# Emission times of the attention scores: two neighbouring groups at one time, from batch 3 on

## The chip, the cores and the metric

The kernel runs on one core of one Trainium2 chip. The metric is the device time of one execution in microseconds (us). The engines are TensorE (PE; its weight loads are shown apart as PEld), VectorE (DVE), ScalarE (ACT), GpSimd (POOL) and SyncE (SP), whose queue issues most of the transfers.

## The reference

Input: q, k, v of shape 8 x 8 x 576 x 64 (batches, heads, positions, head size), and two weights, 512 x 2048 and 2048 x 512. Everything is float32.

```python
scores = scale * q @ k.T                       # per batch and head, 576 x 576
scores = where(0 <= s - t < 128, scores - slope[h] * (s - t), -1e9)
attn = softmax(scores) @ v                     # window of 128 keys, one slope per head
x = heads side by side                         # 8 x 576 x 512
u = x + real(fft(fft(x, axis=1), axis=2))
un = (u - mean(u)) / sqrt(var(u) + 1e-6)       # over the last axis
out = u + max(un @ w_ch1, 0) @ w_ch2
```

## The kernel before

The work of a batch has three stages: attention, the Fourier stage with the normalization (`fourier`, `norm`), and the two FFN products (`ffn`). Three batches are in flight: while the attention of batch b runs, the FFN of batch b - 2 gives TensorE its bulk.

**Attention.** The heads are taken in pairs, four pairs a batch; p = 4b + j counts them through, 0 to 31. The window of 128 keys leaves five tiles of query rows (`TILES`), which form three groups (`SGRP`): group 0 has tiles 1 and 0, group 1 tiles 3 and 2, group 2 tile 4. `scores(p, i)` (line 378) computes group i. From batch 2 on (`NF` = 2) each product of float32 is made of three float16 products, so that a group has 12, 12 or 6 matmuls. Each of them contracts over 64 rows: one head of the pair lies in the upper 64 rows of the array and the other in the lower 64, and they write two PSUM banks, `sp0` and `sp1`. All other matmuls of these batches use the full 128 rows. Pool `ps_s` has two buffers of each bank, that is, two pairs of banks. The other four banks are two for the FFN (`fp`), one for the output of the attention (`pv`) and one for the Fourier stage (`pd`).

Behind a group come, for each of its tiles and heads: a VectorE instruction that adds the bias, masks and takes the row minimum into `nb` (line 391; it is what frees the score bank, and there are four, four or two of them in a group); the exponential on ScalarE; in `halves`, a float16 copy on ScalarE (line 404) and the remainder on VectorE; and in `flip`, a DMA transpose into `pt` on SP's queue (line 413). The tiles `P` have 9 buffers, `pt` 6. `values(p, i, e)` (lines 445 to 447) multiplies `pt` of one head and group with v, and `weigh` divides by the row sum. `convert` makes the float16 halves of q, k and v ahead of a pair.

**FFN.** For each block of 256 positions (odd batches have a third block of 128), FFN1 (line 699) fills an `fp` bank with 24 matmuls of 256 columns (48 of 128 in the small block); ScalarE (line 704) and then VectorE (a helper, line 158, into `hbuf`) take it out and so free the bank. FFN2 (line 713) then runs 48 matmuls of 512 columns for each output tile. `ffn` is a generator that is resumed in 64 steps a batch (80 in odd batches).

**Order.** The order is written as due times: `put(t, f, ...)` lays a call into a heap, `after(dt, ...)` one behind the present time, and the loop at the end takes them out in order of time (calls of one time in the order in which they were put), which is the order of emission. A batch has 24 units of time and a head pair 6. In units from a pair's begin, t: its scores at 0, 2 and 4, its `values` at 5.66 to 10.66, one by one; what follows `scores` is emitted 0.25 to 0.85 units behind it. The FFN of batch b - 2 begins 0.4 units behind the begin of batch b and alternates FFN1 and FFN2 in halves of 6 units (in odd batches 4.8, with the small block at the end). Then the framework's planner goes over the emitted instructions with a simulated clock: on each engine it takes the earliest emitted one whose inputs and buffers are ready by that clock, and so may put a later one ahead. The engines run the planned order strictly, with semaphores for what must wait.

Of the kernel before, what the change touches and what calls it, by code (L numbers as in the profile page):

```python
# [22 lines left out]
NF = 2  # L23
# [32 lines left out]
def begin_of(p):  # L56
    return 6 * PACE[0] * p if p < 4 else T1 + 6 * (p - 4)
# [6 lines left out]
def forward_of(b):  # L64
    return transform_of(b) + (START - DFT if b else 11 * PACE[1])
# [11 lines left out]
def attn_fft_ffn_kernel(  # L77
# [76 lines left out]
    def put(t, f, *a):  # L154
        heappush(queue, (t, next(order), f, a))
# [567 lines left out]
    for p in range(4 * B):  # L723
        b, j = divmod(p, 4)
        t, f = begin_of(p), 1 if b else PACE[0]
        put(t - 7 * f if p else -3.2, load, p)
        if b < NF:
            put(t - 3.8 * f if p else -2, convert, p, 0)
            put(t - 1.2 * f, load_v, p)
            put(t + 4.2 * f, v_max, p)  # L730
        else:
            early = p < 4 * NF + 2
            put(t - (1.3 if early else 6.8), load_v, p)
            for what, x in enumerate((4.6, 3.6, -2 if early else 1.2)):
                put(t - x, convert, p, what)
        for i in range(3):
            put(t + 2 * i * f, scores, p, i)
            for e in range(2 if b < NF else 0):
                put(t + (2 * i + e + LB + 0.33) * f, turn, p, i, e)
        for x in range(6):  # L740
            put(t + (x + LC + 0.66) * f, values, p, x % 3, x // 3)
        if b < NF and j == 3:
            put(t + 5 * f, f32_scale, b)
# [5 lines left out]
    for b in range(B):  # L749
        t = begin_of(4 * b)  # L750
# [4 lines left out]
        t = forward_of(b)  # L755
# [88 lines left out]
def program(q, k, v, moe_w_ch1, moe_w_ch2):  # L844
    import numpy as np
    import concourse.bacc as bacc

    B = q.shape[0]
    qa = np.ascontiguousarray(q.transpose(0, 1, 3, 2)[..., query_order()]).reshape(B, 4, 128, NQ)
    ka = np.concatenate([k, k[:, :, :NK - S]], axis=2).transpose(0, 1, 3, 2)  # L850
    ka = np.ascontiguousarray(ka).reshape(B, 4, 128, NK)
    idx = np.array([[min(s + p, S - 1) for s in VSTART] for p in range(128)])
    va = np.ascontiguousarray(v[:, :, idx])
    nf = min(B, NF)
    v0 = np.ones((nf, H, 128, 5, 65), np.float32)
    v0[..., 0:D] = va[:nf]
    w1 = np.ascontiguousarray(moe_w_ch1.reshape(4, 128, 16, 128).transpose(1, 2, 0, 3).reshape(128, -1))
    w2 = np.ascontiguousarray(moe_w_ch2.reshape(16, 128, DM).transpose(1, 0, 2).reshape(128, -1))
    w1, w2 = w1.view(np.int64), w2.view(np.int64)
    rel, slope, tab1, tab2 = tables()  # L860
    nc = bacc.Bacc("TRN2", target_bir_lowering=False, num_devices=1, dynamic_dma_scratch_size=1024)
    arrays, args = {}, []
    for name, a in (("q", qa), ("k", ka), ("v", va), ("v0", v0), ("w1", w1), ("w2", w2), ("rel", rel),
                    ("slope", slope), ("tab1", tab1), ("tab2", tab2)):
        arrays[name + "_dram"] = a
        args.append(nc.dram_tensor(name + "_dram", a.shape, mybir.dt.from_np(a.dtype), kind="ExternalInput").ap())
    rows = B * S
    args.append(nc.dram_tensor("out_dram", (rows, DM), F32, kind="ExternalOutput").ap())
    with tile.TileContext(nc, schedule_with_timeline_sim=True) as tc:
        attn_fft_ffn_kernel(tc, *args)  # L870
    return nc, arrays, B
```

## Time and profile before

| | |
|---|---|
| median of 3 runs | 1116.77 us (1116.02 to 1118.63) |
| the profiled execution's own time | 1116.72 us |
| span of its profile, first to last instruction | 1114.9 us |
| mean granted TensorE clock | 0.972 |
| busy: PE, DVE, ACT | 1069.6, 712.8, 580.8 us |
| score matmuls (L378), all batches | 880 |
| score reads on VectorE (L391), batches 2 to 7 | 240 |

The profile shows one execution. "L378" is line 378 of the kernel. Busy time of PE is modelled at the ends of matmuls, which are pipelined: two matmuls that follow each other overlap in their rows, so what one costs is read from the start of the next. In rows of waits, the instruction on the left waited for the one behind the arrow. In rows of the time order, "x12" means twelve like instructions merged into one row, with the first one's start and the time to the last one's end; a bracket holds the engine's idle time before it. "out<-in" are the program's tile names, without buffer numbers.

### The profile page before, as it was taken

The page shows a single profiled execution, that of the slowest core. Times are in us where ns is not written, and L with a number is a line of the kernel's source. Part 1 is how long each engine was busy: PE and PEld are TensorE (multiplying, and loading weights), DVE is VectorE, ACT ScalarE, POOL GpSimd, SP SyncE. Part 2 cuts the span into 40 slices and gives each one's busy share as a digit, 9 for nine tenths or more (in the row PEclk, how much of TensorE's full clock was granted, in tenths as well). Part 3 has the DMA queues.
Part 4 walks back from the last instruction along what each step waited for, and adds up shares of the span by engine and source line. Part 5 has one row for each costly group of instructions (what it writes and reads, how often), then busy time and mean ns, then how long its engine had stood idle before and what let it go on. Part 6 is the DMA issues. An engine that isn't in the chain of part 4 may idle for free.

```text
span 1114.9 us, 23952 instructions
## 1 busy us (share of the span) xinstructions
PE 1069.6 (96%) x9296; PEld 737.2 (66%) x9296; DVE 712.8 (64%) x2081; ACT 580.8 (52%) x1380; POOL 20.3 (2%) x59
## 2 busy tenths in 40 slices
PE   6999989879699999999999999999999999999998
PEld 4667768465374857767667677585758577767665
DVE  6988678815966667777868485869685655262111
ACT  5757889647863555446645464456635441151000
POOL 0000000000000000000000000000000000010000
PEclk9999859999899999999999999999999999999999
DMA  9941558656775235432642154344532240020000
GB/s 367 341 153 44 172 131 205 162 156 158 202 145 133 68 82 112 88 97 50 131 106 78 44 110 98 92 77 101 115 83 44 53 89 1 20 48 20 19 11 20
DMA packets 191507, 117.83 MB, mean 106 GB/s; under 512 B 154400, under 2 KB 164128, under 8 KB 191392
## 3 DMA queue, kind: packets, MB, share of 16 engines
q1 hardware_dynamic: 190816, 114.84, 40.8%
q8 instruction: 73, 1.20, 0.5%
q10 hardware_dynamic: 576, 1.45, 0.3%
q14 instruction: 42, 0.34, 0.1%
HBM read 70.63 MB, written 9.44 MB: 72 GB/s over the span
## 4 chain that ended last, share of the span: by engine, by line
PE 69%; DMA 7%; DVE 6%; ACT 3%; issue 1%; SPq 1%; ACTq 0%; DVEq 0%
PE fp L699 29%; PE fp L713 29%; PE sp L378 4%; PE pd L555 2%; DMA pt<-P 2%; DMA wall<-v_dram 2%; DMA wall<-q_dram 2%; ACT wall L257 1%; PE pd L589 1%; PE pv L445 1%; DMA wall<-k_dram 1%; PE pv L447 1%; PE pv L446 1%; DVE P L391 1%; DMA uT<-un 1%
## 5 line engine op out<-in xcount | busy, mean ns | idle before, releaser
L713 PE MATMUL fp<-wall,hbuf 128*128 128x512 f16 x1728 | 397.1, 383 | 2.4 <-DVE hbuf L158 2.3
L699 PEld LDWEIGHTS <-wall 128*128 128x128 f16 x3840 | 340.1, 99 | 61.3 <-issue 14.5
L699 PE MATMUL fp<-uT,wall 128*128 128x256 f16 x3072 | 364.8, 276 | 14.0 <-DVE hbuf L158 8.3
L713 PEld LDWEIGHTS <-hbuf 128*128 128x128 f16 x1728 | 163.2, 99 | 187.2 <-issue 11.5
L158 ACT ACTIVATE P<-P,nb 128x256 f32<-128x256 f32 x320 | 142.9, 479 | 124.6 <-DVE nb L391 124.5
L158 DVE SCALAR_TENSOR_TENSOR hbuf<-fp,hbuf 128x512 f16<-128x512 f32 x144 | 99.0, 688 | 130.4 <-ACT hbuf L704 130.0
L704 ACT ACTIVATE hbuf<-fp 128x512 f16<-128x512 f32 x144 | 85.1, 591 | 186.7 <-PE fp L699 186.5
L391 DVE CUSTOM_DVE_ANT_0 P<-sp,rg,nsl 128x256 f32<-128x256 f32 x240 | 97.3, 450 | 59.7 <-PE sp L378 51.9
L158 DVE SCALAR_TENSOR_TENSOR P<-P 128x256 f16<-128x256 f32 x240 | 88.6, 390 | 26.9 <-ACT P L404 25.6
L378 PE MATMUL sp<-kk,qq 64*128 64x256 f16 (+5 forms) x880 | 93.4, 294 | 11.5 <-DVE nb L391 5.9
L404 ACT ACTIVATE P<-P 128x256 f16<-128x256 f32 x240 | 86.0, 384 | 7.6 <-DMA pt<-P 7.0
L257 ACT ACTIVATE wall<-wall 128x512 f32<-128x512 f32 (+2 forms) x90 | 54.6, 606 | 49.5 <-DMA wall<-v_dram 19.2
L445 PE MATMUL pv<-vhs,pt 128*128 128x65 f16 x432 | 55.5, 195 | 4.6 <-DMA pt<-P 3.4
L446 PE MATMUL pv<-vl,pt 128*128 128x64 f16 x432 | 56.0, 193 | 0.0
L447 PE MATMUL pv<-vhs,pt 128*128 128x65 f16 x432 | 55.9, 194 | 0.0
L158 DVE SCALAR_TENSOR_TENSOR X<-fp,misc,X 128x512 f32<-128x512 f32 x32 | 23.8, 744 | 44.7 <-PE fp L713 44.7
L378 PEld LDWEIGHTS <-qq 64*128 64x128 f16 (+1 forms) x720 | 32.3, 100 | 28.5 <-issue 24.9
L445 PEld LDWEIGHTS <-pt 128*128 128x128 f16 x432 | 41.1, 98 | 15.0 <-issue 4.5
L299 PE MATMUL fp<-tab_sb 128*128 128x512 f16 x180 | 45.5, 379 | 1.1 <-DMA tab_sb<-tab_dram 1.1
L699 PE MATMUL fp<-wall,wall 128*128 128x128 f16 x768 | 45.4, 219 | 0.1
L446 PEld LDWEIGHTS <-pt 128*128 128x128 f16 x432 | 40.7, 99 | 7.0
L440 PE MATMUL pv<-vr,pt 128*128 128x65 f32 x288 | 41.3, 294 | 0.3 <-ACT pt L426 0.3
(146 smaller groups left out, 1200.4 us busy)
## 6 DMA issues: line engine op xcount, KB each, us to landing
qr<-q_dram SPq DMA_DIRECT2D x32, 304.0 KB, 3.1
hbuf<-w_dram SPq DMA_DIRECT2D x16, 512.0 KB, 7.2
out_dram<-X SPq DMA_DIRECT2D x32, 256.0 KB, 2.2
wall<-v_dram SPq DMA_DIRECT2D x30, 256.0 KB, 2.9
vr<-v_dram SPq DMA_DIRECT2D x24, 320.0 KB, 3.6
kr<-k_dram SPq DMA_DIRECT2D x24, 289.0 KB, 3.4
wall<-q_dram SPq DMA_DIRECT2D x24, 256.0 KB, 2.9
wall<-k_dram SPq DMA_DIRECT2D x24, 256.0 KB, 2.9
```

What stands on the lines that cost most here:

```text
L158: put(now[0] + dt, lambda: f(*a, **kw))
L257: A.activation(t, t, AF.Square, accum_out=box["mx"][:, i, c:c + 1])
L299: T.matmul(spin, trig[:, 0:128], trig[:, 0:512], start=True, stop=True)
L378: T.matmul(sp[e][:m, col:col + n], qq[h, c0:c0 + m], keys(kk[h], ti), start=(x == 0), stop=(x == len(prods) - 1))
L391: V.tensor_tensor_reduce(pt[:m, 0:n], sp[e][:m, col:col + n], tab[:m, pc:pc + n], mul, 3.0e38, ALU.add, ALU.min, nb[:m, ti:ti + 1])
L404: A.activation(hi, P32, AF.Copy, scale=2.0 ** 14)
L445: T.matmul(pv[:, ti], ph, vh[:, e, vc], start=first, stop=False)
L446: T.matmul(pv[:, ti, 0:D], ph, vl[:, e, vc], start=False, stop=False)
L447: T.matmul(pv[:, ti], pl, vh[:, e, vc], start=False, stop=last)
L699: T.matmul(fp[:, i * n:(i + 1) * n], w1_ap(e, c, f0 + i), uT[:, j, c, 0:n], start=(c == 0 and p == 0), stop=(c == 3 and p == 2))
L704: A.activation(ht[:, 0], fp, AF.Relu)
L713: T.matmul(op, hh[f][:, a, i * 128:(i + 1) * 128], w2_ap(e, f), start=(f == 0 and p == 0), stop=(f == 15 and p == 2))
```

## The change

```diff
         for i in range(3):
-            put(t + 2 * i * f, scores, p, i)
+            put(t + 2 * i * f + (0 if b < NF + 1 else 1 - 2 * ((3 * p + i) % 2)), scores, p, i)
             for e in range(2 if b < NF else 0):
                 put(t + (2 * i + e + LB + 0.33) * f, turn, p, i, e)
```

From batch 3 on (p = 12), the groups are numbered through as 3p + i. An even group's due time moves one unit later and an odd group's one unit earlier. The groups lay two units apart, so an even group and the odd one behind it now have the same due time: groups 0 and 1 of an even pair p at t + 1, its group 2 and group 0 of pair p + 1 at t + 5, groups 1 and 2 of pair p + 1 at t + 9 (t is the begin of pair p). At these times the even group is emitted first and the odd one directly behind it. What `scores` sends behind itself with `after` moves with it. `values`, `convert`, the loads and the FFN steps keep their due times. 60 groups make 30 such places.

## The prediction

> **What bounds the kernel now.** I read the page first (busy shares and the 40 slices), then stretches of the span, then TensorE's own waits, and only then the order of its instructions.
>
> ```profile
> PE 1069.6 (96%) x9296; PEld 737.2 (66%) x9296; DVE 712.8 (64%) x2081; ACT 580.8 (52%) x1380; POOL 20.3 (2%) x59
> ...
> PE   6999989879699999999999999999999999999998
> ...
> PEclk9999859999899999999999999999999999999999
> ```
>
> TensorE is at nine tenths or more in nearly all slices, against mean shares of 64% and 52% for VectorE and ScalarE. The slices in which PE falls short lie in the first third. Batch 3, where the change begins, starts its scores at 295 us, so the stretches from there on matter (columns: PE, PEld, DVE, ACT and POOL busy, granted clock, DMA share, GB/s):
>
> ```profile
> 299.00:303.00 4.00, 1.43 (x6) 0.86 (x6) 4.00 (x14) 4.00 (x11) 1.22 (x1) 0.53 0.90 259
> 303.00:310.00 7.00, 5.61 (x35) 4.13 (x36) 5.00 (x18) 4.18 (x11) 0.55 (x2) 0.54 1.15 237
> ...
> 340.00:600.00 260.00, 260.00 (x2421) 175.32 (x2420) 188.04 (x561) 133.16 (x317) 4.99 (x12) 1.00 0.41 92
> 600.00:860.00 260.00, 258.71 (x2501) 181.63 (x2500) 184.98 (x550) 136.53 (x322) 4.73 (x11) 1.00 0.39 87
> ```
>
> Two regimes. From 340 us on PE is busy without a hole at the full clock; VectorE has 72% and ScalarE 51% of the stretch. From 299 to 303 us VectorE and ScalarE are full instead, PE starves, and the granted clock stays near 0.53 until 310. TensorE's waits, first for 340 us to the end, then for 295 to 345 us (total us, times, longest), say the same:
>
> ```profile
> PE fp L699 <- DVE X L158: 0.8, 1, 0.8
> PE pv L445 <- DVE X L463: 0.3, 1, 0.3
> PE fp L699 <- DVE hbuf L158: 0.2, 1, 0.2
> ```
> ```profile
> PE sp L378 <- DVE nb L391: 4.9, 1, 4.9
> PE fp L713 <- DVE hbuf L158: 2.3, 1, 2.3
> PE fp L699 <- DVE hbuf L158: 1.9, 2, 1.3
> ```
>
> 1.3 us of waits in 775 us. So in the long stretch only less work for TensorE can shorten the kernel, and "busy" hides what it loses between instructions. That is read from starts. TensorE's order in time (start, duration of the merged row):
>
> ```profile
> 425.02 0.83 PE L378 MATMUL sp<-kk,qq 64*128 64x256 f16 x12
> 425.79 2.85 PE L699 MATMUL fp<-wall,wall 128*128 128x128 f16 x48
> ```
> ```profile
> 436.89 1.46 PE L713 MATMUL fp<-wall,hbuf 128*128 128x512 f16 x6
> 438.28 0.50 PE L378 MATMUL sp<-kk,qq 64*128 64x256 f16 x6
> 438.72 1.47 PE L713 MATMUL fp<-wall,hbuf 128*128 128x512 f16 x6
> 440.02 1.15 PE L699 MATMUL fp<-uT,wall 128*128 128x256 f16 x9
> ```
>
> Six L713 followed by other full-array work take 440.02 - 438.72 = 1.30 us; six followed by scores (L378, 64 rows of the array) take 438.28 - 436.89 = 1.39: 0.09 us on entering. Six scores take 0.44 us until the next instruction, twelve 0.77 (425.02 to 425.79): six more cost 0.33, so 0.11 us of a visit belongs to no matmul, the way out. One visit to the scores costs about 0.09 + 0.10 = 0.19 us (0.20 by the rounded rows; I take the smaller).
>
> [...]
>
> **The change part by part.** No instruction is added or removed: the score matmuls (30 for each head pair, 600 in batches 3 to 7) and what follows them stay. For these batches (20 head pairs, 60 groups) the even-numbered groups are emitted one unit later and the odd ones one earlier, so that two meet at one time, every four units, without other work emitted between them. A unit is 4.92 us here: the first scores of head pairs 16 and 24, 48 units apart, start at 442.92 and 679.00 us.
>
> ```profile
> 295.45 0.67 PE L378 MATMUL sp<-kk,qq 64*128 64x256 f16 x12
> ```
> ```profile
> 442.92 0.28 PE L378 MATMUL sp<-kk,qq 64*128 64x256 f16 x1
> 443.13 2.79 PE L699 MATMUL fp<-uT,wall 128*128 128x256 f16 x24
> 445.86 0.50 PE L378 MATMUL sp<-kk,qq 64*128 64x256 f16 x6
> 446.57 1.47 PE L699 MATMUL fp<-uT,wall 128*128 128x256 f16 x12
> 447.98 0.34 PE L378 MATMUL sp<-kk,qq 64*128 64x128 f16 x5
> ```
> ```profile
> 679.00 0.28 PE L378 MATMUL sp<-kk,qq 64*128 64x256 f16 x1
> ```
> ```profile
> 912.07 0.50 PE L378 MATMUL sp<-kk,qq 64*128 64x256 f16 x6
> ```
>
> *Visits.* Counted along PE's time order, the 600 scores of the 60 groups make 79 visits, the first at 295.45 and the last at 912.07. They are not 60, because the planner cuts groups: the rows show one group of 12 run as 1, 6 and 5, with 24 matmuls (one whole `fp` bank of FFN1 work) and 12 between the pieces. When a bank is not yet free in the plan, scores fill the hole, and older work takes TensorE back. 19 groups are cut, into 21 extra pieces (two neighbours already touch). After the change there are 30 places. If cuts fall by group they halve (41 visits); if they go with the bank changes that a piece of scores meets, all 21 stay (51 visits). The unit arithmetic favours the second: FFN1 and FFN2 halves alternate every 6 units (4.8 in odd batches), and the new places, at 1, 5 and 9 of every 12 units, fall into FFN1 halves two times in three, the groups of before about half the time. I take 51: 28 visits fewer x 0.19 = **-5.3 us**. Bounds: 30 visits (49 x 0.19 = -9.3) and 79 (0). Odd pieces leave one head's half of the array alone; that stays with the cuts, nothing.
>
> *Score banks.* Two buffers of each of `sp0`, `sp1`: a group reuses the banks of the group two before it, four units earlier, as now (19.7 us against the 1.7 us in which VectorE reads a group out, the four rows below), so the second group of a place finds its banks free: nothing. One exception: (12, 1) comes three units after (11, 2) instead of four, and just there PE waits the 4.9 us quoted, with the clock halved. Bounds: that wait vanishes, since the neighbour is emitted with other work now, -4.9; or grows by a whole unit, +4.9. I take 0, since VectorE, which sets it, is full in that stretch with either order.
>
> *Evictions.* Behind a place stand up to eight score reads (L391) on VectorE instead of four, then twice the exponentials on ScalarE, and behind those the evictions of `fp`.
>
> ```profile
> 457.33 0.47 DVE L391 CUSTOM_DVE_ANT_0 P<-sp,rg,nsl 128x256 f32<-128x256 f32 x1
> ...
> 458.54 0.48 DVE L391 CUSTOM_DVE_ANT_0 P<-sp,rg,nsl 96x256 f32<-96x256 f32 x1
> ```
> ```profile
> 443.03 0.60 ACT L704 ACTIVATE hbuf<-fp 128x512 f16<-128x512 f32 x1 [0.48 <-PE fp L699]
> ```
> ```profile
> 443.90 0.68 DVE L158 SCALAR_TENSOR_TENSOR hbuf<-fp,hbuf 128x512 f16<-128x512 f32 x1
> ```
>
> Four reads run from 457.33 to 459.02; four more cost 4 x 0.40 = 1.6 us of VectorE. An `fp` bank is full after 2.6 us (443.13 to 445.86, less the way in); the one full at about 443.0 is free at 444.58, so 1.0 us are spare. If a burst falls wholly on an eviction, PE waits 1.6 - 1.0 = 0.6 us; in 20 places of 30 (those in FFN1 halves) that is +12, the upper bound. Today bursts of four make 0.2 us of this wait in 775 us, and ScalarE and VectorE have 49% and 28% free; nearest to that row I take **+1.0 us** for all new short waits. Less than nothing has no reason here.
>
> *What hangs on the scores.* The exponential, the split and the transposes on SP's queue go with each group: 200 transposes, one unit earlier or later past the loads of q, k and v on the same queue.
>
> ```profile
> 463.83 0.51 PE L378 MATMUL sp<-kk,qq 64*128 64x256 f16 x6
> ```
> ```profile
> 468.55 2.85 SPq L413 DMA_TRANSPOSE pt<-P  x2
> ```
> ```profile
> L413 SPq DMA_TRANSPOSE pt<-P x190: 1167/1200/2446, 350.4 to 916.6; - x190
> ...
> DMA to landing us min/median/max: 2.3/2.4/5.7
> ```
>
> The tightest user is `values` of group 2 of an even head pair: 2.66 units (13.1 us) behind its scores instead of 3.66. The chain took 468.55 + 2.85 + 2.4 - 463.83 = 10.0 us: covered by 3.1. If not, `values` comes later in the plan and FFN matmuls fill in. The largest place queues 8 x 1.2 = 9.6 us of transposes, half of the 19.7 us to the next. `pt` has six buffers and was exactly full; now the last tile of a place waits until `values` frees one, 0.8 unit (4.0 us) later, eight units ahead of its own use. What stands behind it on SP is loads for a head pair not yet begun. All this at nothing; the cost if the cover is gone is a wait of PE of those same 3 to 4 us, once or twice.
>
> **Sum.** The profiled execution took 1116.72 us (span 1114.9, 1.8 around it), the median is 1116.77, so nothing is to be shifted. 1116.7 - 5.3 + 1.0 = **1112.4 us**.
>
> **The rivals.**
> - *More than that* (0.14): cuts halve (38 visits saved, -7.2) and the 4.9 us wait goes: 1104.6. For it: both halves of a place sit in one piece of emission. Against it: FFN1 halves and a full VectorE.
> - *It does not do what it says* (0.17): the planner, which put one group into three pieces, takes the places apart by bank and head, say 70 visits: -1.7, 1115.0, no change that shows. Against it: two groups in three are whole now.
> - *Slower by bursts* (0.16): the 0.6 us above at 20 places, +12, gives 1116.7 - 5.3 + 12 = 1123.4; it outweighs the gain from 0.27 us a place on. For it: places move into the FFN1 halves. Against it: the 0.2 us row. [...]
> - *Slower at the entry* (0.08): (12, 1) waits a unit longer for its bank, +4.9, and the clock stays near 0.53 for as long again, which costs 0.47 x 4.9 = 2.3 of the pace: 1112.4 + 7.2 = 1119.6. The rows at 299 to 310 us speak for it. Against it: the wait is set by VectorE's backlog, not by the place of the scores. [...]
>
> **How the numbers follow.** The forecast holds 0.45, its own range 1109.0 to 1114.5. About 0.2%, 2.2 us, is what a measurement of this kernel tells from no change. Faster: 0.45 + 0.14 = 0.59. Same: 0.17 and a mild form of the bursts, 0.02. Slower: 0.14 + 0.08 = 0.22. From 1104, just under the better case, to 1121, past the entry case, about 0.15 is left out, mostly the full burst case.
>
> **What would show it.** Right: about 50 visits of L378 from batch 3 on, most with 18 or 24 matmuls. L391 in runs of six to eight; the wait for `hbuf` from 340 us on below 2 us; PE at the full clock from 340 us on. Wrong: a row "PE fp L699 <- DVE hbuf L158" of 5 us or more (bursts); 65 visits or more (the planner); a longer "PE sp L378 <- DVE nb L391" with a clock near 0.5 after 310 us (the entry). The forecast fails most easily in the count of cuts and in the 295 to 340 us stretch, where PE waits in any case and a small shift of order can move several us either way.

## The result: slower by 1.3%, and the profile after

| | before | after |
|---|---|---|
| median | 1116.72 us (1116.02 to 1118.63) | 1131.23 us (1129.84 to 1131.86) |
| ratio, 95% interval | | 1.0126 [1.0108, 1.0143] |
| profiled execution, its span | 1116.72, 1114.9 us | 1130.83, 1129.0 us |
| mean granted clock | 0.972 | 0.974 |
| visits to the scores from batch 3 on | 79 | 51 |

The forecast was 1112.4 us with a range up to 1121.0. The kernel lies above both.

The page after, engine shares and slices:

```profile
PE 1064.1 (94%) x9296; PEld 742.2 (66%) x9296; DVE 710.9 (63%) x2081; ACT 583.7 (52%) x1380; POOL 19.6 (2%) x59
...
PE   7999989978789989999999989999899989999998
...
PEclk9999859999799999999999989999999999999999
```

The busy times have hardly changed; TensorE's share fell from 96% to 94%. New is the 8 of the clock in slice 24, far behind the entry of batch 3. The same stretches as before (PE, PEld, DVE, ACT, POOL busy, clock, DMA share, GB/s):

```profile
299.00:303.00 4.00, 1.61 (x10) 1.04 (x10) 4.00 (x13) 4.00 (x10) 1.22 (x1) 0.50 0.97 260
303.00:310.00 7.00, 5.27 (x39) 4.00 (x37) 4.90 (x18) 4.18 (x11) 0.55 (x1) 0.61 1.22 240
...
340.00:600.00 260.00, 254.46 (x2382) 175.62 (x2381) 184.48 (x548) 133.79 (x315) 4.30 (x12) 0.99 0.42 92
600.00:860.00 260.00, 249.96 (x2414) 177.56 (x2413) 181.24 (x545) 134.71 (x317) 4.19 (x11) 0.99 0.37 85
```

The entry is as it was (0.50 and 0.61 for 0.53 and 0.54). The loss is in the stretch in which TensorE had no hole: 5.5 us are missing from 340 to 600 and 8.8 from 600 to 860 (254.46 and 249.96 against 260.00 and 258.71). TensorE's waits, first from 340 us to the end, then the longest from 295 to 345 (total, times, longest):

```profile
PE pv L445 <- DMA pt<-P: 10.5, 3, 4.4
PE fp L699 <- DVE hbuf L158: 2.8, 4, 1.4
PE fp L699 <- DVE X L158: 2.7, 3, 1.7
PE fp L699 <- DVE pm L515: 2.3, 1, 2.3
PE fp L713 <- DVE hbuf L158: 1.3, 2, 0.9
```
```profile
PE sp L378 <- DVE nb L391: 5.4, 1, 5.4
```

19.6 us of waits from 340 on, where there were 1.3. More than half is one row that did not exist before: `values` (L445) waiting for the transposed exponentials `pt`, three times. The two long waits of that row (4.36 us ending at 424.53, 4.24 us at 665.24) are for group 2, first head, of head pairs 14 and 22; the third (1.90 us at 800.10) is for group 1 of the odd pair 27.

To set this against the gain, TensorE's time from the first score of batch 3 to its last instruction is divided up in both traces. Each distance from one start to the next is compared with the median of the same form of instruction before. What is over goes to "scores" (all distances that begin at a score, and the extra time on entering), to waits, or to the clock at half speed:

| us | visits | scores | waits | half clock | all other | sum |
|---|---|---|---|---|---|---|
| before | 79 | 49.1 | 13.1 | 4.0 | 749.3 | 815.5 |
| after | 51 | 43.0 | 33.1 | 5.8 | 748.5 | 830.3 |

28 visits fewer gave 6.1 us, 0.22 us a visit; the waits took 20.0 and the half clock 1.8. The sum of +14.8 us answers to the +14.1 of the two profiled executions.

One place shows how the new wait comes about. It lies in the last FFN1 half of an odd batch, that of the small block, when two of its four `fp` fillings are issued ("the seam" from here on), and the values are those of group 2 of head pair 22. TensorE before, and SP's queue:

```profile
643.22 0.50 PE L378 MATMUL sp<-kk,qq 64*128 64x256 f16 x6
...
660.83 0.19 PE L445 MATMUL pv<-vhs,pt 128*128 128x65 f16 x1
```
```profile
646.74 2.51 SPq L413 DMA_TRANSPOSE pt<-P  x2
```

The same after: TensorE, SP's queue, ScalarE, VectorE.

```profile
650.62 0.72 PE L378 MATMUL sp<-kk,qq 64*128 64x256 f16 x10
652.05 0.45 PE L378 MATMUL sp<-kk,qq 64*128 64x256 f16 x8
659.84 1.16 PE L378 MATMUL sp<-kk,qq 64*128 64x256 f16 x18
665.24 0.23 PE L445 MATMUL pv<-vhs,pt 128*128 128x65 f16 x1 [4.24 <-DMA pt<-P]
```
```profile
662.78 5.11 SPq L413 DMA_TRANSPOSE pt<-P  x4
```
```profile
656.30 0.90 ACT L158 ACTIVATE P<-P,nb 128x256 f32<-128x256 f32 x2
...
658.43 1.50 ACT L158 ACTIVATE P<-P,nb 128x256 f32<-128x256 f32 x4
659.81 0.72 ACT L404 ACTIVATE P<-P 128x256 f16<-128x256 f32 x2
660.42 0.59 ACT L704 ACTIVATE hbuf<-fp 128x512 f16<-128x512 f32 x1
```
```profile
662.29 0.76 DVE L158 SCALAR_TENSOR_TENSOR P<-P 128x256 f16<-128x256 f32 x2
...
664.16 0.67 DVE L158 SCALAR_TENSOR_TENSOR hbuf<-fp,hbuf 128x512 f16<-128x512 f32 x1
...
665.09 0.68 DVE L158 SCALAR_TENSOR_TENSOR hbuf<-fp,hbuf 128x512 f16<-128x512 f32 x1
```

Before, the first transpose starts at 646.74 and lands 2.7 us later, at 649.5; the values run at 660.83, so 11.3 us are spare. After, the scores run 650.62 - 643.22 = 7.4 us later, and from the scores to the first transpose 12.2 us pass instead of 3.5: the two tiles, read out by VectorE from 651.4 on, get their exponentials on ScalarE at 656.30, behind other work, and the neighbour's four exponentials stand ahead of the split. The transpose lands at 665.2, 15.7 us later than before. TensorE comes to the values at 661.00, nearly when it did before: 4.2 us too early, and the row shows 4.24. And there is nothing to fill the hole: the FFN banks are full, and VectorE frees them at 664.83 and 665.77 (the ends of its last two rows for `hbuf`), behind the same backlog. The wait is put down to `pt`, but at that moment the banks were late as well. The place at 411 to 425 us is the same picture (4.36).

### The profile page after: what moved, and what is told of

Read it like the earlier page. It is cut to its first block, busy times and chain, and to the rows that moved or that the text cites. A ratio compares the mean times of both kernels' runs of the same rounds, so it can differ in the third digit from the quotient of the medians.

```text
span 1129.0 us, 23955 instructions
## 1 busy us (share of the span) xinstructions
PE 1064.1 (94%) x9296; PEld 742.2 (66%) x9296; DVE 710.9 (63%) x2081; ACT 583.7 (52%) x1380; POOL 19.6 (2%) x59
## 4 chain that ended last, share of the span: by engine, by line
PE 63%; DVE 13%; DMA 10%; ACT 9%; issue 3%; SPq 1%; POOL 0%; DVEq 0%; ACTq 0%
PE fp L713 26%; PE fp L699 23%; DMA pt<-P 4%; PE sp L378 4%; PE fp L299 3%; PE pd L555 2%; DVE P L391 2%; ACT wall L257 2%; DMA wall<-k_dram 2%; DMA wall<-q_dram 2%; DMA wall<-v_dram 2%; PE pv L440 1%; ACT P L158 1%; DVE P L158 1%; ACT wall L216 1%
## 5 line engine op out<-in xcount | busy, mean ns | idle before, releaser
L713 PE MATMUL fp<-wall,hbuf 128*128 128x512 f16 x1728 | 393.0, 382 | 3.3 <-ACT P L404 1.8
L699 PEld LDWEIGHTS <-wall 128*128 128x128 f16 x3840 | 342.9, 99 | 67.3 <-issue 21.5
L699 PE MATMUL fp<-uT,wall 128*128 128x256 f16 x3072 | 361.8, 275 | 17.3 <-DVE hbuf L158 11.1
L158 ACT ACTIVATE P<-P,nb 128x256 f32<-128x256 f32 x320 | 139.9, 479 | 61.6 <-DVE nb L391 60.8
L378 PE MATMUL sp<-kk,qq 64*128 64x256 f16 (+5 forms) x880 | 88.3, 295 | 11.5 <-DVE nb L391 6.0
L445 PE MATMUL pv<-vhs,pt 128*128 128x65 f16 x432 | 56.7, 196 | 15.0 <-DMA pt<-P 13.9
L445 PEld LDWEIGHTS <-pt 128*128 128x128 f16 x432 | 41.3, 98 | 24.5 <-DMA pt<-P 14.9
L699 PE MATMUL fp<-wall,wall 128*128 128x128 f16 x768 | 48.4, 229 | 4.0 <-DVE pm L515 2.3
L299 PE MATMUL fp<-tab_sb 128*128 128x512 f16 x180 | 48.0, 396 | 1.1 <-DMA tab_sb<-tab_dram 1.1
L378 PEld LDWEIGHTS <-qq 64*128 64x128 f16 (+1 forms) x720 | 33.2, 100 | 21.4 <-issue 17.6
L446 PEld LDWEIGHTS <-pt 128*128 128x128 f16 x432 | 40.9, 99 | 6.8
L447 PEld LDWEIGHTS <-pt 128*128 128x128 f16 x432 | 41.2, 99 | 0.8
```

The costliest lines, as they stand in the source:

```text
L158: put(now[0] + dt, lambda: f(*a, **kw))
L299: T.matmul(spin, trig[:, 0:128], trig[:, 0:512], start=True, stop=True)
L378: T.matmul(sp[e][:m, col:col + n], qq[h, c0:c0 + m], keys(kk[h], ti), start=(x == 0), stop=(x == len(prods) - 1))
L445: T.matmul(pv[:, ti], ph, vh[:, e, vc], start=first, stop=False)
L446: T.matmul(pv[:, ti, 0:D], ph, vl[:, e, vc], start=False, stop=False)
L447: T.matmul(pv[:, ti], pl, vh[:, e, vc], start=False, stop=last)
```

## The experiments

Each kernel was timed beside the kernel before on the same chip; times differ from run to run by some us, much of it ahead of batch 3 (its first score starts at 288.0 to 299.4 us in the traces), so waits are compared from 340 us on. The offsets of the even and odd groups, written (even, odd) in units, are (0, 0) before and (1, -1) after. "Waits" below are TensorE's from 340 us on, summed over the rows of the view.

**values_later.** Are the values simply due too early?

```diff
-            put(t + (x + LC + 0.66) * f, values, p, x % 3, x // 3)
+            put(t + (x + LC + 0.66) * f + (0.9 if b > NF and p % 2 == 0 and x == 2 else 0), values, p, x % 3, x // 3)
```

> The changed kernel, but the values of group 2, first head, of even head pairs are due 0.9 unit later too, so that they stand 3.56 units behind their scores instead of 2.66. Lateness theory (TensorE stands still at values whose group was scored a unit later while the values kept their place): the wait of PE at L445 for the transposes, 10.5 us in the changed kernel from 340 us on, falls below 3 us, the clock stays full there, and the time falls from 1131 to 1117 to 1121 us. Burst theory (eight score reads in a row, nine P buffers and blocked queues of ScalarE and VectorE make the loss): at most 3 us of the 14 come back, 1128 us or more.

1134.39 us, ratio 1.0170 [1.0124, 1.0215].

```profile
PE pv L445 <- DMA pt<-P: 10.6, 3, 4.4
```

The same three waits at the same places, with as many FFN1 matmuls still to come (2976, 2016 and 1488) as in the changed kernel. So the later due time did not move these values in TensorE's order: at the seam the planner has nothing else that it could put there. Whether later values would help is not shown by this run.

**both_earlier.** Pairs at the even group's old place, (0, -2).

```diff
-            put(t + 2 * i * f + (0 if b < NF + 1 else 1 - 2 * ((3 * p + i) % 2)), scores, p, i)
+            put(t + 2 * i * f + (0 if b < NF + 1 else (0, -2)[(3 * p + i) % 2]), scores, p, i)
```

> Groups are still brought together two by two, but the odd one comes two units earlier and the even one stays, so that no group is scored later than in the kernel before. Lateness theory: about 50 visits of TensorE to the scores, a wait at L445 below 3 us, and 1110 to 1118 us: the saved visits, 6 us, less what the bursts cost. Burst theory: the bursts are the same and the buffers are held even longer, 1126 us or more.

1113.09 us, ratio 0.9995 [0.9965, 1.0026]; 46 visits, waits 6.1 us.

```profile
PE fp L699 <- DVE hbuf L158: 3.5, 8, 1.0
PE fp L713 <- DVE hbuf L158: 2.0, 1, 2.0
PE fp L699 <- DVE X L158: 0.6, 1, 0.6
```

The pairs are there, with fewer visits than in the changed kernel, and the loss is not. What differs is one unit of the place.

**even_alone, odd_alone.** Each half of the change alone, (1, 0) and (0, -1); no two groups meet, and the distances are 1 and 3 units.

```diff
-            put(t + 2 * i * f + (0 if b < NF + 1 else 1 - 2 * ((3 * p + i) % 2)), scores, p, i)
+            put(t + 2 * i * f + (0 if b < NF + 1 else (1, 0)[(3 * p + i) % 2]), scores, p, i)  # even_alone
+            put(t + 2 * i * f + (0 if b < NF + 1 else (0, -1)[(3 * p + i) % 2]), scores, p, i)  # odd_alone
```

> One part of the change alone: even groups one unit later, odd groups unmoved, so that no two groups meet. Lateness theory: the visits stay at 70 to 85 and the wait at L445 appears without any meeting, 5 to 11 us, 1121 to 1130 us. Burst theory: without a meeting no burst, 1114 to 1119 us.

> The other part alone: odd groups one unit earlier, even groups unmoved; no two groups meet and none is later. Both theories: 70 to 85 visits, a wait at L445 below 3 us, 1113 to 1120 us. A time above 1122 us would speak against both: then any shift of the scores disturbs the order.

even_alone 1123.59 us, 1.0077 [1.0043, 1.0111], waits 11.5; odd_alone 1120.76, 1.0043 [1.0022, 1.0065], waits 10.8. Rows of even_alone:

```profile
PE fp L699 <- DVE hbuf L158: 10.6, 8, 4.5
PE pv L445 <- DMA pt<-P: 0.6, 1, 0.6
```

Both halves cost, and together (0.77% + 0.43%) about what the change costs. But they are not the parts of its waits: group 2 is due as late in even_alone as in the change, and the wait for `pt` is 0.6 us instead of 10.5, against what was expected of lateness. odd_alone has no such wait at all; both wait mostly for `hbuf`.

**not_at_tail, only_at_tail.** The change for the first eight of a batch's twelve groups, and for the last four alone.

```diff
-            put(t + 2 * i * f + (0 if b < NF + 1 else 1 - 2 * ((3 * p + i) % 2)), scores, p, i)
+            put(t + 2 * i * f + (0 if b < NF + 1 or (3 * p + i) % 12 >= 8 else (1, -1)[(3 * p + i) % 2]), scores, p, i)  # not_at_tail
+            put(t + 2 * i * f + (0 if b < NF + 1 or (3 * p + i) % 12 < 8 else (1, -1)[(3 * p + i) % 2]), scores, p, i)  # only_at_tail
```

> Four of the six meetings of a batch stay (units 1, 5, 9 and 13), the two at units 17 and 21, where VectorE and ScalarE also do the end of the Fourier stage and the normalization, are undone. Collision theory (the meetings at the tail add their burst to a backlog of VectorE and ScalarE, evictions of fp come up to 8 us late, TensorE runs out of work): PE waits from 340 us on fall from 19.6 to below 6 us, about 60 visits, time 1110 to 1117 us. Rival, meetings cost anywhere by their bursts: two thirds of the loss stay, 1124 to 1129 us.

> The complement: only the two meetings at units 17 and 21 of each batch are made. Collision theory: most of the loss stays although only a third of the meetings do, PE waits of 12 us or more, 1122 to 1132 us. Rival, meetings cost anywhere: a third of the loss, 1118 to 1122 us. An early slot alone without its late one elsewhere may add or take 3 us in either.

not_at_tail 1120.13 us, 1.0035 [1.0008, 1.0062], waits 8.0; only_at_tail 1125.04, 1.0072 [1.0045, 1.0098], waits 12.0. Each part has a share of the loss, with more of it at the batch's end. That 8.0 + 12.0 is nearly the 19.6 is no proof of a simple sum, for neither run waits for `pt` from 340 us on. only_at_tail gives the groups at the seam the due times of the change, and TensorE runs the same 18 scores there (from 649.68 us); the first transpose follows 10.0 us behind them, but TensorE waits 1.55 us for an `fp` bank, fills it with 48 more FFN1 matmuls, and then finds the values ready. So the late chain becomes a wait for `pt` only together with the order that the planner makes around it.

**buffers, both_earlier_buffers.** Two more `P` tiles (room made by one `ut` tile laid elsewhere), with (1, -1) and with (0, -2).

```diff
-PB = 9
+PB = 11
-                uts[b // 2] = xp.tile([128, DM], F32, name="ut", bufs=2)
+                uts[b // 2] = wall[1][:, 8, 512:1024] if b % 4 else xp.tile([128, DM], F32, name="ut", bufs=1)
```

> The changed kernel with 11 buffers of P instead of 9; the room is made by laying every second ut tile into a part of the weight tile that is free by then. Buffer theory (score reads and splits stand in VectorE's and ScalarE's queues until transposes give P buffers back, and the evictions stand behind them): the waits of L391 and L404 for transposes, 31.8 us from 340 us on, fall below 8, PE waits fall by 5 us or more, 1118 to 1126 us. Collision theory without a part for the buffers: the waits of L391 and L404 fall, but PE's stay at 16 us or more and the time within 3 us of 1131.

> Meetings made by moving only the odd groups, two units earlier, with 11 buffers of P: the same 45 to 50 visits, more room. If buffers count, the PE waits of 6.1 us of the version with 9 buffers fall to 3 and the time lies 2 to 4 us under that one, about 1109 to 1112; if not, it stays within 2 us of it, 1111 to 1115.

buffers 1134.13 us, 1.0133 [1.0095, 1.0170]; both_earlier_buffers 1125.84, 1.0059 [1.0039, 1.0080], slower than with nine tiles. Rows of buffers:

```profile
PE fp L699 <- DVE hbuf L158: 8.8, 8, 3.0
PE pv L445 <- DMA pt<-P: 6.8, 3, 4.2
```

More `P` tiles are no cure. The waits of lines 391 and 404 for transposes, which they were to take away, fell from 31.8 to 19.4 us only, and TensorE's rose from 19.6 to 21.8; that too few tiles have no part in it is not shown. That more of them cost 0.6% at (0, -2) (waits 13.7 instead of 6.1, nearly all for `hbuf`) shows how strongly any shift of the order acts on these waits.

**light_after, light_before.** Is the seam overloaded by the Fourier stage? Both leave out the last 33 rows of its second step from batch 2 on, some 2 us of ScalarE and 2.7 us of VectorE a batch.

```diff
+            if j == 2 and b >= NF:
+                return                                   # cols_out
...
+            if j == 2 and b >= NF:
+                V.tensor_copy(ut[p0:p0 + 32], X2[0:32])  # cols_add
+                V.tensor_copy(ut[p0 + 64:p0 + 96], X2[64:96])
+                return
```

> The changed kernel without the last 33 rows of the Fourier stage from batch 2 on: the five ScalarE instructions that take them out and five of the seven VectorE instructions that add them are left out (two copies stand in for the rest; its output is not the reference's). That takes some 2 us of ScalarE and 2.7 us of VectorE out of the tail of each batch and nothing out of TensorE. Collision theory (the meetings at units 17 and 21 add their burst to the backlog of VectorE and ScalarE in that tail): the PE waits from 340 us on fall from 19.6 to below 10 us and the time by 8 us or more, to 1114 to 1123 us. Rival, the loss is one of the planner's order alone, which sends TensorE to waiting work wherever it lies: within 4 us of 1131.

> The same left out of the kernel before, as the control. Both theories: PE hardly waits there, so the time stays within 3 us of the kernel before, 1112 to 1119 us; a larger gain would mean that the left-out work costs TensorE something without any meeting.

light_after 1130.30 us, 1.0143 [1.0107, 1.0180], waits 17.3 (9.0 of them for `pt`); light_before 1115.27, 1.0003 [0.9976, 1.0029], waits 1.7. The load of that work alone is not the cause either.

**earlier_still, both_earlier_again.** Pairs two units ahead of the change's place, (-1, -3), and (0, -2) once more, with more executions.

```diff
-            put(t + 2 * i * f + (0 if b < NF + 1 else 1 - 2 * ((3 * p + i) % 2)), scores, p, i)
+            put(t + 2 * i * f + (0 if b < NF + 1 else (-1, -3)[(3 * p + i) % 2]), scores, p, i)  # earlier_still
+            put(t + 2 * i * f + (0 if b < NF + 1 else (0, -2)[(3 * p + i) % 2]), scores, p, i)  # both_earlier_again
```

> Meetings at units -1, 3, 7, 11, 15 and 19 of a batch: even groups one unit earlier, odd ones three. Collision theory: what counts is where the meetings lie in the tail (18 to 22); one at 19 with four or six tiles, none at 17 or 21: PE waits from 340 us on between 4 and 12 us, about 48 visits, 1111 to 1120 us. Rival, any order unlike the old one costs the same: 1124 us or more.

> The version with meetings at 0, 4, 8, 12, 16 and 20 once more, with more rounds: by its saved visits, 6.9 us, less its PE waits, 6.1 against 1.3 us, it should lie 1 to 4 us under the kernel before, a ratio of 0.996 to 0.999. A ratio of 1.000 or more would say that the profile's gain is lost in the first 340 us.

earlier_still 1129.46 us, 1.0117 [1.0078, 1.0155], waits 17.6, though every group is earlier than in the kernel before. both_earlier_again 1113.89, 0.9986 [0.9964, 1.0007], waits 6.8. So being late is not all of it: one unit of the place decides, in both directions, and at the good place the pairs gain at most what a measurement can tell.

**after_spread, row_only, bursts_only.** Here the two sides of a pair are taken apart: the matmuls on TensorE, and the reads with all that follows on the other engines. In `scores` the part from `nb` on becomes `reads()`, and is emitted 2 units later for one kind of group.

```diff
+        def reads():
             for e in range(2):
                 ...
+        if b > NF and (3 * p + i) % 2:          # bursts_only: == 0
+            after(2.0, reads)
+        else:
+            reads()
```

after_spread has the matmuls at (1, -1) and the reads at (1, 1); row_only (0, -2) and (0, 0); bursts_only (-1, -1) and (1, -1). Lines behind 383 lie 6 lower in these kernels (L451 is `values`, L705 FFN1, L719 FFN2).

> The change, with one thing taken back: the odd group's score matmuls stay directly behind the even group's, but its reads by VectorE (L391), its exponentials, splits and transposes are emitted 2 units later, so that the two groups of a place no longer pile their follow-up work on VectorE and ScalarE at one time. Burst theory (the 18 us of new waits of TensorE come from the two groups' follow-up work standing together ahead of the evictions of the FFN banks): about 51 visits as in the changed kernel, TensorE's waits from 340 us on below 8 us instead of 19.6, time 1112 to 1120. Order theory (the waits come from TensorE's own order: FFN banks filled without scores between them, so that no filler stands at the bank changes, whatever the two other engines do): waits stay at 15 us or more, time 1126 or more.

> Only TensorE's part of the change: the odd group's matmuls are emitted 2 units earlier, directly behind the even group's, and nothing else is moved; the reads, exponentials, splits and transposes of all groups keep the due times of the kernel before. Burst theory: about 46 to 51 visits, waits of TensorE from 340 us on of 1 to 5 us, time 1109 to 1113, that is the 5 to 6 us of the visits term without their price. Order theory: waits of 6 us or more, time 1113 to 1118.

> Only the other part: the matmuls of the groups stay two units apart as in the kernel before (all one unit earlier), but the even group's reads and what follows them are emitted 2 units late, so that VectorE and ScalarE get the follow-up work of two groups at the places and in the pairs of the changed kernel. Burst theory: about 79 visits as before, TensorE's waits from 340 us on of 12 us or more, time 1128 to 1135. Order theory: waits of 1 to 4 us, time 1114 to 1119.

after_spread 1128.98 us, 1.0154 [1.0124, 1.0184]; row_only 1112.85, 0.9993 [0.9968, 1.0019]; bursts_only 1118.53, 1.0048 [1.0029, 1.0067]. The longest rows of waits of the three, in that order:

```profile
PE pv L451 <- DMA pt<-P: 4.7, 2, 2.4
PE fp L705 <- DVE X L158: 3.5, 3, 2.0
```
```profile
PE fp L705 <- DVE hbuf L158: 3.4, 1, 3.4
PE fp L705 <- DVE X L158: 1.2, 2, 0.8
```
```profile
PE fp L705 <- DVE hbuf L158: 4.4, 5, 1.2
PE pv L451 <- DMA pt<-P: 3.0, 2, 2.9
```

Neither theory holds for all three. Spreading the reads took the waits from 19.6 only to 14.2 us and gave no time back (in the table below, the scores take 3.5 us more and the half clock 4.1), against the burst theory. Matmuls in a row cost 3 us of waits at row_only's place, against the order theory, and 14 at after_spread's, which is the same kernel one unit later. What was left to try was that unit by itself.

**late_all, early_all.** All groups one unit later, or earlier; nothing is paired.

```diff
-            put(t + 2 * i * f + (0 if b < NF + 1 else 1 - 2 * ((3 * p + i) % 2)), scores, p, i)
+            put(t + 2 * i * f + (0 if b < NF + 1 else 1), scores, p, i)  # late_all
+            put(t + 2 * i * f + (0 if b < NF + 1 else -1), scores, p, i)  # early_all
```

> The kernel before with all score groups of batches 3 to 7 emitted one unit later, still two units apart: no two groups meet, only their place against the FFN halves, the converts and the values moves. Row_only and after_spread are the same kernel but for one unit of that place, and TensorE waits 4.6 us in the one and 14.2 in the other from 340 us on. Place theory (the unit in which the scores and their reads fall against the FFN halves sets the waits, pairing little): waits of TensorE from 340 us on of 8 us or more, time 1121 to 1130, about 79 visits. Pairing theory (the waits need two groups at one place): waits of 1 to 4 us, time 1112 to 1118.

> The kernel before with all score groups of batches 3 to 7 emitted one unit earlier, still two units apart. Bursts_only has the same matmuls and reads the even groups two units later, and waits 9.8 us from 340 us on. Place theory: since both places of the phase two units apart fall on the odd units of the row of FFN halves, waits of 6 us or more, time 1118 to 1126. Pairing theory: waits of 1 to 4 us, time 1111 to 1117, and the difference to bursts_only is what the reads in pairs cost.

late_all 1120.17 us, 1.0077 [1.0047, 1.0108], waits 11.4; early_all 1117.43, 1.0055 [1.0032, 1.0079], waits 8.5. The longest row of early_all, the waits of late_all, then late_all's order of TensorE in time at the seam shown above:

```profile
PE fp L713 <- ACT hbuf L704: 4.9, 2, 3.9
```
```profile
PE fp L699 <- DVE hbuf L158: 4.5, 3, 3.4
PE pv L445 <- DMA pt<-P: 4.4, 2, 2.2
PE fp L699 <- DVE X L158: 2.5, 2, 1.3
```
```profile
643.99 0.50 PE L378 MATMUL sp<-kk,qq 64*128 64x256 f16 x6
651.83 1.33 PE L378 MATMUL sp<-kk,qq 64*128 64x256 f16 x24
655.40 0.20 PE L445 MATMUL pv<-vhs,pt 128*128 128x65 f16 x1 [2.24 <-DMA pt<-P]
```

The same wait at the same seam, without a pair having been asked for. Counted by the FFN1 matmuls still to come, TensorE waits for `pt` with 2976 and with 2016 left in the changed kernel (4.36 and 4.24 us), in after_spread (2.38, 2.34) and in late_all (2.13, 2.24); in row_only, both_earlier and the kernel before it does not. (The 24 scores in a row at 651.83 are the planner's doing: it had put off one group until the next was due.)

All versions side by side (sums as in the table above):

| matmuls | reads | kernel | visits | scores | waits from 340 | half clock | sum | ratio |
|---|---|---|---|---|---|---|---|---|
| (0, 0) | (0, 0) | before | 79 | 49.1 | 1.3 | 4.0 | 815.5 | 1 |
| (0, -2) | (0, 0) | row_only | 47 | 42.6 | 4.6 | 4.3 | 810.6 | 0.9993 |
| (0, -2) | (0, -2) | both_earlier | 46 | 42.1 | 6.1 | 1.9 | 810.7 | 0.9995 |
| (1, 1) | (1, 1) | late_all | 61 | 45.3 | 11.4 | 4.9 | 820.8 | 1.0077 |
| (1, -1) | (1, 1) | after_spread | 53 | 46.5 | 14.2 | 9.9 | 831.4 | 1.0154 |
| (1, -1) | (1, -1) | after | 51 | 43.0 | 19.6 | 5.8 | 830.3 | 1.0126 |
| (-1, -1) | (-1, -1) | early_all | 67 | 46.1 | 8.5 | 4.1 | 817.3 | 1.0055 |
| (-1, -1) | (1, -1) | bursts_only | 66 | 46.8 | 10.1 | 3.4 | 821.0 | 1.0048 |

- *The place*: one unit later costs 10.1 us of waits with groups apart (before to late_all), 9.6 in a row (row_only to after_spread), 13.5 for whole pairs (both_earlier to after). In time, 0.8% apart and 1.3 to 1.6% in a row.
- *The row on TensorE*: 3.3 us of waits at the old place, 2.8 one unit later. At the old place the saved visits pay for it and the time stays; one unit later it comes with a further 0.8%, in which the half clock has a part (9.9 against 4.9 us).
- *The reads in pairs*: 1.5, 5.4 and 1.6 us of waits in the three comparisons, and no time that shows (0.9993 to 0.9995, 1.0154 to 1.0126, 1.0055 to 1.0048; all intervals overlap).

## Why the prediction was wrong

**Visits: the number right, the picture only in part.** 51 forecast, 51 counted; -5.3 us forecast, -6.1 measured, 0.22 us a visit instead of 0.19 (the other versions in the table give 0.10 to 0.25). But only 12 of the 51 visits have 18 or 24 matmuls, where the prediction expected most to have them: the planner takes apart more places than it leaves whole. And the cuts do not simply stay: the same 30 places give 46 visits in both_earlier and 53 in after_spread, and groups apart 60 to 79. That it came to exactly 51 is partly luck.

**Score banks and the entry: right.** 0 forecast; the wait at 301 us is 5.4 instead of 4.9 us, and the clock from 303 to 310 is 0.61 instead of 0.54.

**Evictions: too small, but not the main thing.** +1.0 us was forecast for all new short waits. The two rows for `hbuf` from 340 us on hold 2.8 + 1.3 = 4.1 us, those behind other VectorE work (`X`, `pm`) 5.0. The step behind the number, 20 places at 0.6 us each as the upper end, did not describe it: these are ten waits of 0.3 to 2.3 us, five of them longer than 0.6. The mark for right, `hbuf` below 2 us, was missed, and the clock was not full throughout.

**What hangs on the scores: here it failed.** For the two long waits the prediction found the right user, group 2 of an even head pair with 2.66 units (13.1 us) to its values, and even the right price, "a wait of PE of those same 3 to 4 us, once or twice": 4.36 and 4.24 us. It took this as nothing because a chain at a quiet place (463.83 to 473.8 us) took 10.0 us. At the seam it takes 14.6 us (650.62 to 665.2) until just the first transpose has landed, and TensorE comes to the values 10.4 us behind the scores (650.62 to 661.00), not 13.1. So the cover of 13.1 - 10.0 = 3.1 us was 10.4 - 14.6 = -4.2 us: the chain was 4.6 us longer, and the distance on TensorE 2.7 us shorter than that of the due times. The chain was measured at one place and used for all 30; it is longer at the seam, where the conversions, the normalization, the Fourier outputs and the neighbour's exponentials stand on the same two engines. The three waits for `pt` are 10.5 us, more than half of the new ones (the third, 1.9 us, is at a user that the prediction did not name). The fallback, that "FFN matmuls fill in", failed too: both `fp` banks were full and waited for the same two engines. In only_at_tail it held, at the price of 1.55 us.

**What the sum left out.** The due times moved by one unit against the FFN halves, and that by itself had no term. late_all pairs nothing and costs 0.77%. The prediction compared the places with the halves only to count cuts, and so took the place for free.

**The rivals.** "Slower by bursts" had the right sign, and with 1123.4 us came nearest; its mechanism is not borne out. after_spread takes the reads apart and gains no time, and the row it named, `fp` waiting for `hbuf` at L699, stayed at 2.8 us, under its mark of 5. "Slower at the entry" is excluded by the 5.4 us. "Does not do what it says" is wrong in its time and, by the 51 visits against its mark of 65, in its count, though the planner did take most places apart, as it says. None of the rivals stood for a `pt` that comes late.

What stays open: why the place of before is good in both directions. For one unit later the seam rows show part of it, 4.4 of late_all's 11.4 us of waits. For one unit earlier the longest wait of early_all is another one (the 3.9 us for ScalarE's `hbuf`, at 897 us), and its cause is not shown. How much of each shift is the place itself, and how much is the planner's new order around it, the runs do not separate: even_alone and only_at_tail have the late group 2 and hardly a wait for `pt`, and both_earlier lost 0.6% by two buffers that it had in addition.

## What to carry to other kernels

When a change moves due times, price the move against the stages that run beside it, before the thing that the move is for: here a unit without any pairing cost 0.8%, more than the whole saving of 0.5%. Take the length of a chain at the place where its engines are fullest, not where it is easily read (here 14.6 against 10.0 us); a distance of due times is not yet one on the engine (13.1 against 10.4 us). And before saying that other work fills a hole, look whether that work has a free bank just there. A wait that names a transfer can hide a second one that ends at nearly the same time; then the first alone is not the whole price, as at the seam, where the first of the banks came free 0.4 us before `pt`. And see that an experiment moved what it was to move: in values_later the values kept their place in TensorE's order.

## What the runs showed of the hardware

The half clock did not follow the length of a wait alone. Stretches of late_all, around its waits of 2.24 us (ending at 655.40) and 3.45 us (the 3.60 of the third row less 0.15 busy); the sixth value behind the span is the clock:

```profile
653.00:655.40 2.40, 0.16 (x5) 0.01 (x1) 2.40 (x7) 0.00 (x0) 0.00 (x0) 1.00 0.51 141
655.40:659.40 4.00, 4.00 (x46) 4.00 (x47) 3.33 (x20) 2.30 (x7) 0.92 (x1) 0.57 0.33 68
896.40:900.00 3.60, 0.15 (x3) 0.06 (x2) 2.13 (x8) 2.89 (x6) 0.00 (x0) 1.00 0.45 93
900.00:904.00 4.00, 4.00 (x55) 3.29 (x56) 4.00 (x15) 3.25 (x9) 0.00 (x0) 1.00 0.50 96
```

The shorter wait was followed by 0.57 for 4 us, the longer one by the full clock. In the traces of the kernel before and of the changed one, the clock stands at half for 3.41, 6.83, 10.24 or 27.31 us at a time (the last stretch, cut by the end of the trace, apart), and its changes lie whole multiples of 3.413 us apart: in the changed kernel such stretches begin at 137.85, 298.27, 424.57 and 663.50 us, 47, 37 and 70 multiples from one to the next. For late_all an estimate follows: 0.57 over 4.00 us is 2 x 0.43 x 4.00 = 3.4 us at half, one such stretch, begun between 655.59 (up to there the values follow each other every 0.03 us, as before the wait) and 655.99 (3.41 us ahead of the row's end). The shorter wait, 653.16 to 655.40, then lay whole in the 3.41 us before it, with TensorE busy for 3.41 - 2.24 = 1.17 of them; the longer one was divided 71 multiples on, between 897.94 and 898.34, with at most 1.94 us of it in the stretch before and 2.06 in the one behind. The runs give no sharp limit of the busy time: in the changed kernel 3.41 us with 1.67 us busy (663.50 to 666.91) were followed by 3.41 us more at half, and 3.41 us with 1.57 busy (796.62 to 800.03) by the full clock. In the changed kernel both waits above 4 us went with half clock, 3.4 us of it from 424.6 and 6.8 us from 663.5.
